# Attention's weights split into float16 halves from the fourth tile of tokens on, and integer additions issued in pieces of 256 columns

## The chip, the core and the metric

The kernel runs on one core of a Trainium2 chip. The metric is device time in microseconds (us): 732.31 us, the median of three runs (731.12 to 734.42). The core's engines each work through a queue of their own, in order: PE (TensorE: matmuls, and PEld, its weight loads), DVE (VectorE), ACT (ScalarE), POOL (GpSimd). SP issues all DMAs here.

## The reference

Attention that keeps the 32 largest scores of a row, followed by two feed-forward layers; batch 2, 8 heads, 576 tokens, head size 64, so 1152 tokens of 512 numbers.

```python
scores = scale * np.matmul(q, k.transpose(0, 1, 3, 2))
kth = np.partition(scores, -top_k, axis=-1)[..., -top_k:-top_k + 1]
scores = np.where(scores >= kth, scores, -1000000000.0)
attn = np.exp(scores - np.max(scores, axis=-1, keepdims=True))
attn = attn / (np.sum(attn, axis=-1, keepdims=True) + 1e-09)
x = np.matmul(attn, v)                      # then [tokens, 512]
h = x @ w_in;  x = np.maximum(0.01 * h, h) @ w_out          # 512 -> 2048 -> 512
h = x @ w2_in; out = (h * np.tanh(softplus(h))) @ w2_out    # 512 -> 2048 -> 512
```

All inputs and the output are float32.

## The kernel before

**Tiles and slots.** The 1152 tokens are nine tiles of 128 (0 to 8). A slot is one head of one tile: 72 slots, in order of tile and then head. Tile 4 holds the end of batch 0 and the start of batch 1, 64 tokens each, so what is a matmul over 128 tokens elsewhere is two over 64 there.

**One slot.** `front` makes the scores (2 halves of 288 columns, L469, into one PSUM bank of `ps_s`) and ACT copies them out (L471). `topk` finds the 32nd largest score on DVE: four MAX8 (L484) and three MATCH_REPLACE8 (L487), each over 576 columns. `weigh` computes three small numbers on POOL (L502 to L506), and ACT makes the masked exponentials `e` (L509, L510). `back` multiplies `e` by V, for which `e` must be transposed:

- `back` in float32 (tiles 0 to 4): PE transposes four blocks of 128 columns into a bank of `ps_pt` (L520), ACT copies them out (L521), PE transposes the last 64 columns (L524), ACT copies those (L525), and five float32 matmuls follow (L529), each recorded as two.
- `back16` (tiles 5 to 8, `T16 = 5`): ACT copies `e` to its float16 half (L542), POOL subtracts for the second half (L543), one DMA transposes both (L546, into `pts`), and PE runs 15 float16 matmuls (L553 to L555). The halves lie in one of two buffers `eh` by turns, 640 columns each, padded with zeros; `pts` comes from the pool `kvp`, which also holds V. This path needs V as float16 halves too: `split_v` makes them in place, per pair of heads, on ACT (squares L124, scaling L363, rounding L365) and POOL (L366). Before, only batch 1's V is split, from slot 34 on (`VX = 34`; `VS = 98` for batch 0 is past the last slot).

**Weights.** The four weight matrices arrive as float32 in 16 groups (`load_w`, slots -1 to 15; `split_w` one slot later), and are brought into a scaled form and float16 halves. A group's first step shifts and joins the words as integers: DVE L209, L212, L215 and L220, and on POOL additions L213 and L218 of 1024 (at the end 512) columns.

**Feed-forward.** A step is `first` (48 matmuls of 128 columns, L609 to L611) of one quarter of a layer for a tile, and `second` (12 of 512 columns, L618 to L620). There are 72 steps; one or two go with a slot from slot 6 on, the rest follow the last slot.

**Order.** The program is written slot by slot with priorities (`at(i, late)`), and a list scheduler with its own timing places every instruction; pools of tiles with few buffers add waits. Pools that matter here: `kvp` with `VB = 5` buffers (V, and `pts` of tiles 5 to 8), `krp` with one, `qp` with one (the queries' float16 halves `qn`, tiles 0 to 4), `sp1` with one (`pts` of `back`). The names `aside` are two scratch rows for `split_v` and for batch 1's K: one lies in the weights' arena, the other is a tile of its own.

Of the kernel before, what the change touches and what calls it, by code (L numbers as in the profile page):

```python
# [18 lines left out]
def topk_attention_moe_moe2_kernel(  # L19
# [34 lines left out]
    VB = 5  # L54
    LV = 0
# [96 lines left out]

    CV = (2, 1, 1, 2, 2, 1, 1, 1, 1, 1, 1, 1, 1, 1, 0, 1)
# [37 lines left out]
    def load_w(q):  # L191
# [4 lines left out]
        for c, n, k0 in stages:  # L196
# [11 lines left out]
            for o, lo, hi in runs:  # L208
                nc.vector.tensor_scalar(out=o, in0=hi, scalar1=3, scalar2=0x3FFFFFFF, op0=ALU.logical_shift_left,  # L209
                                        op1=ALU.bitwise_and)  # L210
                if CV[q] == 2:
                    nc.vector.tensor_scalar(out=hi, in0=hi, scalar1=-0x40000000, scalar2=None, op0=ALU.bitwise_and)  # L212
                    nc.gpsimd.tensor_tensor(out=o, in0=o, in1=hi, op=ALU.add)  # L213
# [90 lines left out]
    def load_kv(src, pool, tag, b, hp):  # L304

        t = pool.tile([P, 2, NB, D], F32, tag=tag, name="raw" + tag)
        nc.sync.dma_start(
            out=t[:, :, 0:4, :],
            in_=src[b, 2 * hp:2 * hp + 2, 0:4 * P, :].rearrange("h (p i) d -> p h i d", i=4))
        for to, at0, n in (((0, S - P, P),) if src is k else ((0, S - SREM, SREM), (SREM, S - P, P - SREM))):  # L310
            nc.sync.dma_start(out=t[to:to + n, :, 4, :],
                              in_=src[b, 2 * hp:2 * hp + 2, at0:at0 + n, :].rearrange("h p d -> p h d"))
        return t

    asides = [warena[:, 4 * NCHW * CH + NB * P:4 * NCHW * CH + NB * P + NB * D],
              cpool.tile([P, NB * D], F32, name="aside")]
# [34 lines left out]
    def split_v(b, hp):  # L351
# [3 lines left out]
        for h in range(2):  # L355
            a = asides[h]
# [3 lines left out]
        for h in range(2):  # L360
            a = asides[h]
# [29 lines left out]
    def prep_q(t, qr):  # L391
# [46 lines left out]
    class Tile_:  # L438
# [11 lines left out]
        def front(self, h):  # L450
# [11 lines left out]
            for half in range(2):  # L462
                where, tag = ((ps_s, "s"), (ps_pt, "pt"))[half if self.t >= SB else 0]
# [48 lines left out]
        def back(self, h):  # L512
# [9 lines left out]
            where, tag = ((ps_pt, "pt"), (ps_g, "g"))[self.t >= TG]  # L522
            pu = where.tile([P, 512], F32, tag=tag, name="pu")
# [8 lines left out]
        def back16(self, h, e):  # L532

            hp, hh = divmod(h, 2)
            if not ehs:
                ehs.append(wh[:, 4 * NCHW * 2 * CH:4 * NCHW * 2 * CH + 2 * SP].rearrange("p (c n) -> p c n", c=2))
                t = krp.tile([P, 2, NB, D], F32, tag="kr", name="eh")
                ehs.append(t.rearrange("p a b c -> p (a b c)").bitcast(F16).rearrange("p (c n) -> p c n", c=2))
                for eh in ehs:
                    nc.gpsimd.memset(eh[:, :, S:], 0.0)  # L540
# [4 lines left out]
            ph = pts.rearrange("p a b c -> p (a b c)").bitcast(F16).rearrange("p (n q) -> p n q", q=P)  # L545
            nc.sync.dma_start(out=ph, in_=eh.rearrange("p c n -> p (c n)"), transpose=True)  # L546
            for b, s, n, p0 in tokens(self.t):
                o = self.av[p0:p0 + n, h * D:(h + 1) * D]
                for i, r in enumerate(R):
                    first, last = i == 0, i == NB - 1  # L550
                    pa, pb = [ph[:r, c * NB + i, p0:p0 + n] for c in range(2)]
                    va, vb = [vsp[b, hp][:r, hh, c, i, :] for c in range(2)]
                    nc.tensor.matmul(o, lhsT=pa, rhs=va, start=first, stop=False)  # L553
                    nc.tensor.matmul(o, lhsT=pa, rhs=vb, start=False, stop=False)
                    nc.tensor.matmul(o, lhsT=pb, rhs=va, start=False, stop=last)  # L555
# [44 lines left out]
    def product_in(m, hi, lo, g, t):  # L600
        where, tag = ((ps_m, "m"), (ps_pt, "pt"))[t >= MB and g == 3]
# [51 lines left out]
    class Layer:  # L653
# [11 lines left out]
        def first(self, g):  # L665
            ph = product_in(2 * self.l, self.hi, self.lo, g, self.t)
# [161 lines left out]
    for i in range(-2, NS):  # L828
# [38 lines left out]
    n = NS  # L867
    while todo or late:
# [33 lines left out]
```

## Time and profile before

| | |
|---|---|
| median of three runs | 732.31 us |
| profiled execution | 732.71 us, of it the span 730.9 us |
| PE busy | 645.2 us (88%) |
| DVE busy | 561.2 us (77%) |
| ACT busy | 541.1 us (74%) |
| POOL busy | 394.0 us (54%) |
| mean granted clock of PE | 0.962 of 2.4 GHz |
| chain that ended last | PE 41%, DVE 23%, ACT 12%, DMA 8% |

The span is the time from the first to the last instruction; 1.8 us of the execution lie outside it. A share of busy time is a mean over stages with different limits, so the stages are to be read apart. They are: the weights with tiles 0 to 2 (until about 285 us), tiles 3 and 4 (until about 423 us), tiles 5 to 8 (until about 630 us), and the feed-forward steps that are left.

### The profile page before, as it was taken

Reading aid. Unit: us, or ns where it says so; the run is one execution under the profiler, and the core shown is the slowest. Engines: PE = TensorE matmul, PEld = TensorE weight load, DVE = VectorE, ACT = ScalarE, POOL = GpSimd, SP = SyncE. Lnnn points to the kernel's source line nnn. Section 1 sums busy time; section 2 is a strip of 40 time slices with the busy share of each in tenths; the row PEclk is TensorE's granted clock in tenths of the full one; section 3 lists DMA queues with packets and bytes.
Section 4 is the critical chain, followed back from the end, with each engine's and each line's share of the span. In section 5 each row is a group of like instructions: output and inputs, shape, how many; then the busy total and the mean of one; then the engine's idle time right before and its main releaser. Section 6 shows DMA issues by size and latency. Waiting matters only on the chain.

```text
span 730.9 us, 16578 instructions
## 1 busy us (share of the span) xinstructions
PE 645.2 (88%) x6428; PEld 464.6 (64%) x6428; DVE 561.2 (77%) x1184; ACT 541.1 (74%) x1056; POOL 394.0 (54%) x550
## 2 busy tenths in 40 slices
PE   2389589888959999899999989998999989999996
PEld 1255345556648776677677757767767767677772
DVE  4998989999899788978687689788889899220112
ACT  5398688888786889877888696786797688663543
POOL 2648855667874754333255465466566557533230
PEclk9999889999976999999999998998999999999998
DMA  8842445351522112002212123233335334310000
GB/s 291 279 163 86 168 167 170 116 155 40 193 90 73 59 37 50 2 23 44 51 36 58 23 54 73 64 69 74 78 60 103 73 57 65 70 30 17 1 16 29
DMA packets 92367, 60.45 MB, mean 83 GB/s; under 512 B 78848, under 2 KB 82944, under 8 KB 92288
## 3 DMA queue, kind: packets, MB, share of 16 engines
q1 hardware_dynamic: 92288, 59.39, 30.1%
q8 instruction: 50, 0.82, 0.5%
q14 instruction: 29, 0.24, 0.1%
HBM read 41.16 MB, written 2.36 MB: 60 GB/s over the span
## 4 chain that ended last, share of the span: by engine, by line
PE 41%; DVE 23%; ACT 12%; issue 8%; DMA 8%; POOL 6%; SPq 1%; POOLq 0%; DVEq 0%; ACTq 0%
DVE top L484 6%; PE ph L609 5%; DVE wk L487 5%; PE ph L610 5%; PE ph L611 5%; PE y L618 5%; PE y L619 5%; PE y L620 5%; PE av L529 3%; PE sps L469 2%; DVE warena L215 2%; DVE warena L209 2%; DMA warena<-in_moe_w_out_dram 2%; DMA pts<-warena 2%; DMA warena<-in_moe_w_in_dram 2%
## 5 line engine op out<-in xcount | busy, mean ns | idle before, releaser
L609 PE MATMUL ph<-xt,warena 128*128 128x128 f16 x1152 | 204.7, 221 | 1.4 <-DMA xt<-xp 1.4
L610 PE MATMUL ph<-xt,warena 128*128 128x128 f16 x1152 | 204.5, 221 | 0.0
L611 PE MATMUL ph<-xt,warena 128*128 128x128 f16 x1152 | 204.5, 221 | 0.0
L484 DVE MAX8 top<-wk 128x8 f32<-128x576 f32 x216 | 157.5, 749 | 1.3
L610 PEld LDWEIGHTS <-warena 128*128 128x128 f16 x1152 | 114.0, 99 | 8.4 <-issue 2.5
L609 PEld LDWEIGHTS <-warena 128*128 128x128 f16 x1152 | 114.3, 99 | 7.9 <-issue 1.1
L618 PE MATMUL y<-warena,gl 128*128 128x512 f16 x288 | 110.9, 385 | 6.0 <-POOL gl L648 2.8
L611 PEld LDWEIGHTS <-warena 128*128 128x128 f16 x1152 | 114.1, 99 | 2.8 <-issue 1.1
L619 PE MATMUL y<-warena,gh 128*128 128x512 f16 x288 | 110.7, 384 | 0.0
L620 PE MATMUL y<-warena,gh 128*128 128x512 f16 x288 | 110.7, 384 | 0.0
L487 DVE MATCH_REPLACE8 wk<-top,wk 128x576 f32<-128x576 f32 x144 | 106.7, 741 | 0.0
L218 POOL TENSOR_TENSOR warena<-warena 128x1024 int32<-128x1024 int32 x26 | 64.1, 2468 | 31.8 <-DVE warena L215 9.1
L509 ACT ACTIVATE wk<-sc,nb,iv 128x576 f32<-128x576 f32 x72 | 62.5, 868 | 20.4 <-POOL nb L502 20.3
L484 DVE MAX8 top<-sc 128x8 f32<-128x576 f32 x72 | 54.0, 750 | 28.6 <-ACT sc L471 27.6
L471 ACT COPY sc<-sps 128x288 f32<-128x288 f32 x144 | 56.9, 395 | 25.0 <-PE sps L469 24.9
L469 PE MATMUL sps<-kst,qst 128*128 128x288 f16 (+1 forms) x320 | 64.7, 304 | 9.5 <-ACT sc L471 5.0
L529 PEld LDWEIGHTS av<-rawkv,pts 128*128 128x128 f32 (+3 forms) x480 | 56.3, 183 | 15.0 <-issue 3.7
L529 PE MATMUL av<-rawkv,pts 128*128 128x64 f32 (+3 forms) x480 | 64.5, 270 | 1.2 <-ACT pts L525 1.2
L502 POOL TENSOR_SCALAR nb<-top,iv 128x1 f32<-128x1 f32 x72 | 21.8, 302 | 80.5 <-DVE top L484 60.1
L645 DVE SCALAR_TENSOR_TENSOR mc<-mc,hs 128x512 f32<-128x512 f32 x36 | 26.1, 725 | 50.4 <-ACT mc L644 50.4
L510 ACT ACTIVATE wk<-wk,nb 128x576 f32<-128x576 f32 x72 | 55.9, 777 | 6.2 <-POOL nb L506 5.9
L632 POOL TENSOR_TENSOR gl<-lk,gh 128x512 f16<-128x512 f32 x36 | 43.6, 1210 | 27.4 <-ACT lk L631 27.0
(179 smaller groups left out, 1481.8 us busy)
## 6 DMA issues: line engine op xcount, KB each, us to landing
warena<-in_moe_w_in_dram SPq DMA_DIRECT2D x16, 1024.0 KB, 5.4
warena<-in_moe_w_out_dram SPq DMA_DIRECT2D x11, 1024.0 KB, 4.9
warena<-in_moe_w_out_dram SPq DMA_DIRECT2D x10, 512.0 KB, 3.4
out_dram<-o SPq DMA_DIRECT2D x9, 256.0 KB, 2.0
qr<-in_q_dram SPq DMA_DIRECT2D x8, 256.0 KB, 3.2
rawkv<-in_v_dram SPq DMA_DIRECT2D x8, 256.0 KB, 2.8
rawkr<-in_k_dram SPq DMA_DIRECT2D x6, 256.0 KB, 3.2
rawkv<-in_k_dram SPq DMA_DIRECT2D x2, 256.0 KB, 7.8
```

The lines of the kernel that those rows point to most:

```text
L218: nc.gpsimd.tensor_tensor(out=o, in0=o, in1=lo, op=ALU.add)
L469: nc.tensor.matmul(sps[p0:p0 + n, :HS], lhsT=lq[:, c, p0:p0 + n], rhs=rk[:, half * HS:(half + 1) * HS], start=(c == 0), stop=(c == 1))
L484: queued(nc.vector.max(out=top[:, 8 * r:8 * r + 8], in_=src))
L487: queued(nc.vector.match_replace(out=wk, in_to_replace=top[:, 8 * r:8 * r + 8], in_values=src, imm_value=NEG))
L509: nc.scalar.activation(e, sc, AF.Prelu, bias=nb[:, 0:1], scale=iv, alpha=1e30)
L529: nc.tensor.matmul(o, lhsT=pts[:r, i, p0:p0 + n], rhs=vst[b, hp][:r, hh, i, :], start=(i == 0), stop=(i == NB - 1))
L609: nc.tensor.matmul(o, lhsT=wb, rhs=xa, start=(c == 0), stop=False)
L610: nc.tensor.matmul(o, lhsT=wa, rhs=xb, start=False, stop=False)
L611: nc.tensor.matmul(o, lhsT=wa, rhs=xa, start=False, stop=(c == KC - 1))
L618: nc.tensor.matmul(y, lhsT=gb, rhs=whi(j), start=(g == 0 and f == 0), stop=False)
L619: nc.tensor.matmul(y, lhsT=ga, rhs=wlo(j), start=False, stop=False)
L620: nc.tensor.matmul(y, lhsT=ga, rhs=whi(j), start=False, stop=(g == FG - 1 and f == 3))
```

## The change

- `T16` goes from 5 to 3: tiles 3 and 4, 16 slots, take `back16`. Batch 0's V is therefore split too, at slots 18 to 24 (`VS = 18`), and batch 1's from slot 30 on (`VX = 30`).
- In `back16` the two halves lie without padding, the last 64 columns of both in one block, so that the DMA moves 9 blocks of 128 instead of 10 and a head has 14 matmuls instead of 15; POOL's subtraction becomes two instructions. In tiles 3 and 4 (`TK = 5`) there is one `eh` and one `pts` (of `sp1`); from tile 5 on `eh` alternates between two as before, and `pts` comes from `kvp`.
- `kvp` has 6 buffers instead of 5. Room for it comes from `aside`: its second row is now the buffer `qn` of the queries.
- POOL's integer additions are issued in pieces of 256 columns (`add`).
- `SB` goes from 99 to 3: from tile 3 on the second half of a head's scores uses a bank of `ps_pt`, as it does for the very first head. The feed-forward uses that bank for its fourth quarter only once the last slot has been written (`over`), not from tile 7 on.

```diff
-    VB = 5
-    LV = 0
+    VB = 6
+    LV = 2
+    PIECE = 256
+    def add(o, x):
+        for a in range(0, o.shape[1], PIECE):
+            nc.gpsimd.tensor_tensor(out=o[:, a:a + PIECE], in0=o[:, a:a + PIECE], in1=x[:, a:a + PIECE], op=ALU.add)
...
-                    nc.gpsimd.tensor_tensor(out=o, in0=o, in1=lo, op=ALU.add)
+                    add(o, lo)
...
-    asides = [warena[:, 4 * NCHW * CH + NB * P:4 * NCHW * CH + NB * P + NB * D],
-              cpool.tile([P, NB * D], F32, name="aside")]
+    def aside(h):
+        if h:
+            return qp.tile([P, 6 * P], F16, tag="qn", name="aside").bitcast(F32)[:, :NB * D]
+        return warena[:, 4 * NCHW * CH + NB * P:4 * NCHW * CH + NB * P + NB * D]
...
-                where, tag = ((ps_s, "s"), (ps_pt, "pt"))[half if self.t >= SB else 0]
+                where, tag = ((ps_s, "s"), (ps_pt, "pt"))[half if self.t >= SB or (self.t, h) == (0, 0) else 0]
...
         def back16(self, h, e):
-            eh = ehs[h % 2]
-            nc.scalar.copy(eh[:, 0, :S], e)
-            nc.gpsimd.tensor_tensor(out=eh[:, 1, :S], in0=e, in1=eh[:, 0, :S], op=ALU.subtract)
-            pts = kvp.tile([P, 2, NB, D], F32, tag="kv", name="pts")
+            if self.t < TK or h % 2:
+                eh = wh[:, 4 * NCHW * 2 * CH:4 * NCHW * 2 * CH + 2 * S]
+            else:
+                if not ehs:
+                    ehs.append(krp.tile([P, 2, NB, D], F32, tag="kr", name="eh"))
+                eh = ehs[0].rearrange("p a b c -> p (a b c)").bitcast(F16)[:, :2 * S]
+            nc.scalar.copy(eh[:, :S], e)
+            nc.gpsimd.tensor_tensor(out=eh[:, S + SREM:], in0=e[:, :4 * P], in1=eh[:, :4 * P], op=ALU.subtract)
+            nc.gpsimd.tensor_tensor(out=eh[:, S:S + SREM], in0=e[:, 4 * P:], in1=eh[:, 4 * P:S], op=ALU.subtract)
+            if self.t < TK:
+                pts = sp1.tile([P, NB, P], F32, tag="pts", name="pts").rearrange("p a b -> p (a b)")
+            else:
+                pts = kvp.tile([P, 2, NB, D], F32, tag="kv", name="pts").rearrange("p a b c -> p (a b c)")
...
-    T16 = 5
-    TG = 5
-    VS = 98
-    VX = 34
+    T16 = 3
+    TK = 5
+    VS = 18
+    VX = 30
...
-    SB = 99
+    SB = 3
```

Three places in the order of the instructions. First POOL at the weights' first groups; L213 and L218 are the additions, L158 is the line of `add`. Before:

```order
L455 TENSOR_SCALAR iv<-ki,qi 128x2
L458 TENSOR_SCALAR iv<-iv 128x2
L213 TENSOR_TENSOR warena<-warena 128x1024
L218 TENSOR_TENSOR warena<-warena 128x1024
L213 TENSOR_TENSOR warena<-warena 128x1024
L218 TENSOR_TENSOR warena<-warena 128x1024 x2
L455 TENSOR_SCALAR iv<-ki,qi 128x2
L218 TENSOR_TENSOR warena<-warena 128x1024
```

With the change:

```order
L465 TENSOR_SCALAR iv<-ki,qi 128x2
L468 TENSOR_SCALAR iv<-iv 128x2
L158 TENSOR_TENSOR warena<-warena 128x256 x20
L465 TENSOR_SCALAR iv<-ki,qi 128x2
L158 TENSOR_TENSOR warena<-warena 128x256 x4
L468 TENSOR_SCALAR iv<-iv 128x2
```

Five additions of 1024 columns became twenty of 256 in the same place.

Second, ACT at the fifth and sixth head of tile 3. Line numbers of the change stand 10 to 16 higher. Before, with the two copies per head (L521, L525):

```order
L509 ACTIVATE wk<-sc,nb,iv 128x576
L521 COPY pts<-pt 128x512
L510 ACTIVATE wk,sums<-wk,nb 128x576
L430 COPY qst<-qt 128x1024
L471 COPY sc<-sps 128x288
L630 ACTIVATE gh<-ph,fac_1115 128x512
L631 ACTIVATE lk<-ph,fac_1115 128x512
L686 ACTIVATE o<-y,ivo 128x512
L525 COPY pts<-pu 64x128
```

With the change (L551 is the copy to float16):

```order
L702 ACTIVATE o<-y,ivo 128x512
L519 ACTIVATE wk<-sc,nb,iv 128x576
L551 CAST warena<-wk 128x576
L520 ACTIVATE wk,sums<-wk,nb 128x576
L124 ACTIVATE qn,qpart<-qr 128x512
L646 ACTIVATE gh<-ph,fac_1180 128x512
L647 ACTIVATE lk<-ph,fac_1180 128x512
L519 ACTIVATE wk<-sc,nb,iv 128x576
L417 ACTIVATE qn<-qr,qs 128x4x64
L551 CAST warena<-wk 128x576
```

The second CAST writes the same part of `warena` as the first, which the DMA transpose reads in between; six other instructions stand between the two.

Third, SP at tile 3. `kst` are the transposes of batch 1's K, `pts` those of the weights. Before:

```order
L307 DMA rawkr<-in_k_dram 128x2x256
L311 DMA rawkr<-in_k_dram 128x2x64
L340 DMA_TRANSPOSE kst<-warena 128x4x128
L342 DMA_TRANSPOSE kst<-warena 128x64
L340 DMA_TRANSPOSE kst<-aside 128x4x128
L342 DMA_TRANSPOSE kst<-aside 128x64
```

With the change:

```order
L559 DMA_TRANSPOSE pts<-warena 128x9x128
L398 DMA qr<-in_q_dram 64x8x64 x2
L559 DMA_TRANSPOSE pts<-warena 128x9x128 x2
L350 DMA_TRANSPOSE kst<-warena 128x4x128
L559 DMA_TRANSPOSE pts<-warena 128x9x128
L352 DMA_TRANSPOSE kst<-warena 128x64
L350 DMA_TRANSPOSE kst<-aside 128x4x128
L352 DMA_TRANSPOSE kst<-aside 128x64
```

Sixteen transposes of `pts` now stand among the loads and transposes of batch 1's K and the queries.

## Rows read from the trace of the kernel before

**Rows 1.** Windows: us, then busy us (instructions) per engine, clock, DMA, GB/s.
```profile
20.00:240.00 220.00, 172.79 (x1204) 117.99 (x1205) 208.69 (x409) 170.28 (x302) 145.26 (x146) 0.91 0.41 138
240.00:420.00 180.00, 174.58 (x1833) 131.08 (x1831) 143.10 (x333) 145.19 (x324) 83.88 (x154) 1.00 0.16 39
420.00:625.00 205.00, 195.41 (x2328) 145.02 (x2327) 181.47 (x386) 160.50 (x321) 126.08 (x205) 0.97 0.36 69
```

**Rows 2.** Instructions by line, DVE, 10 to 262 us: busy us, mean ns | idle.
```profile
L209 DVE TENSOR_SCALAR warena<-warena 128x1024 int32<-128x1024 int32 (+1 forms) x30 | 35.6, 1187 | 7.6 <-PE lp L256 2.8 <-DMA warena<-in_moe_w_in_dram 2.4 <-DMA warena<-in_moe_w_out_dram 2.3
L215 DVE SCALAR_TENSOR_TENSOR warena<-warena 128x1024 int32<-128x1024 int32 (+1 forms) x24 | 33.6, 1401 | 0.2
...
L212 DVE TENSOR_SCALAR warena<-warena 128x1024 int32<-128x1024 int32 x6 | 7.0, 1168 | 0.1
```

**Rows 3.** Timeline of DVE: start us, us, instruction [idle before].
```profile
12.45 0.69 DVE L209 TENSOR_SCALAR warena<-warena 128x1024 int32<-128x1024 int32 x1 [1.29 <-DMA warena<-in_moe_w_in_dram]
...
23.05 1.23 DVE L215 SCALAR_TENSOR_TENSOR warena<-warena 128x1024 int32<-128x1024 int32 x1
...
71.38 2.89 DVE L209 TENSOR_SCALAR warena<-warena 128x1024 int32<-128x1024 int32 x1
```

**Rows 4.** Line L218 on POOL: ns min/median/max, first and last start.
```profile
L218 POOL TENSOR_TENSOR warena<-warena x26: 2369/2397/2847, 16.4 to 191.2; 128x1024 int32<-128x1024 int32 x26
L218 POOL TENSOR_TENSOR wraw<-wraw,warena x8: 1289/1302/1626, 194.3 to 255.7; 128x512 int32<-128x512 int32 x8
```

**Rows 5.** Timeline of PE, tile 3: `back` in float32.
```profile
328.20 0.27 PE L524 MATMUL pu<-identf,wk 128*64 128x128 f32 x1
328.31 1.00 PE L529 MATMUL av<-rawkv,pts 128*128 128x64 f32 x8
329.15 0.22 PE L610 MATMUL ph<-xt,warena 128*128 128x128 f16 x1
...
330.44 0.43 PE L529 MATMUL av<-rawkv,pts 64*128 64x64 f32 x2
330.80 0.66 PE L520 MATMUL pt<-identf,wk 128*128 128x128 f32 x4
331.30 0.22 PE L611 MATMUL ph<-xt,warena 128*128 128x128 f16 x1
```

**Rows 6.** Timeline of PE, tile 5: the 15 matmuls of `back16`, first and next.
```profile
445.20 0.19 PE L553 MATMUL av<-rawkv,pts 128*128 128x64 f16 x1
...
445.84 0.23 PE L609 MATMUL ph<-xt,warena 128*128 128x128 f16 x1
```

**Rows 7.** Instructions by line, ACT, whole span.
```profile
L521 ACT COPY pts<-pt 128x512 f32<-128x512 f32 x40 | 23.3, 583 | 10.5 <-PE pt L520 10.0 <-PE av L529 0.3
L542 ACT CAST warena<-wk 128x576 f16<-128x576 f32 x16 | 10.8, 673 | 0.1
L525 ACT COPY pts<-pu 64x128 f32<-64x128 f32 x40 | 10.3, 258 | 10.1 <-PE pu L524 10.0
L363 ACT ACTIVATE warena<-rawkv,vs 128x320 f32<-128x320 f32 x4 | 2.3, 573 | 0.0
L124 ACT ACTIVATE warena<-rawkv 128x320 bf16<-128x320 f32 x4 | 1.9, 470 | 1.7 <-DMA rawkv<-in_v_dram 1.3 <-DVE top L484 0.4
L365 ACT CAST rawkv<-warena 128x320 f16<-128x320 f32 x4 | 1.8, 461 | 0.0
```

**Rows 8.** Timeline of ACT: exponentials of the first head of tiles 3 and 5.
```profile
284.93 0.76 ACT L510 ACTIVATE wk<-wk,nb 128x576 f32<-128x576 f32 x1
...
423.36 0.78 ACT L510 ACTIVATE wk<-wk,nb 128x576 f32<-128x576 f32 x1
```

**Rows 9.** DMA issues: count, median us to landing.
```profile
pts<-warena SPq DMA_TRANSPOSE x16, 3.5
```

**Rows 10.** Instructions by line, POOL: the subtraction of `back16`.
```profile
L543 POOL TENSOR_TENSOR warena<-wk,warena 128x576 f16<-128x576 f32 x16 | 21.6, 1348 | 22.6 <-ACT warena L542 22.3
```

**Rows 11.** Waits, 420 to 625 us: who <- for whom: us, times, longest.
```profile
PEld L553 <- DMA pts<-warena: 9.5, 7, 3.0
```

More of the change, by code (lines that the diff above doesn't have):

```diff
@@ L212, in load_w @@
                     nc.vector.tensor_scalar(out=hi, in0=hi, scalar1=-0x40000000, scalar2=None, op0=ALU.bitwise_and)
-                    nc.gpsimd.tensor_tensor(out=o, in0=o, in1=hi, op=ALU.add)
+                    add(o, hi)
                 else:
@@ L309, in load_kv @@
             in_=src[b, 2 * hp:2 * hp + 2, 0:4 * P, :].rearrange("h (p i) d -> p h i d", i=4))
-        for to, at0, n in (((0, S - P, P),) if src is k else ((0, S - SREM, SREM), (SREM, S - P, P - SREM))):
+        for to, at0, n in (((0, S - P, P),) if src is k else ((0, S - SREM, SREM), (SREM, S - SREM, SREM))):
             nc.sync.dma_start(out=t[to:to + n, :, 4, :],
@@ L355, in split_v @@
         for h in range(2):
-            a = asides[h]
+            a = aside(h)
             squares(raw[:, h].rearrange("p i d -> p (i d)"), part[:, h:h + 1], a.bitcast(BF16)[:, :NB * D])
@@ L360, in split_v @@
         for h in range(2):
-            a = asides[h]
+            a = aside(h)
             r = raw[:, h].rearrange("p i d -> p (i d)")
@@ L400, in prep_q @@
             else:
-                qn = qp.tile([P, 4, 3, D], F16, tag="qn", name="qn").rearrange("p a b c -> p (a b c)")
+                qn = qp.tile([P, 6 * P], F16, tag="qn", name="qn")
             if not c:
@@ L521, in back @@
             nc.scalar.copy(pts[:, 0:4, :], pt)
-            where, tag = ((ps_pt, "pt"), (ps_g, "g"))[self.t >= TG]
-            pu = where.tile([P, 512], F32, tag=tag, name="pu")
+            pu = ps_pt.tile([P, 512], F32, tag="pt", name="pu")
             nc.tensor.transpose(pu[:SREM, :P], e[:, 4 * P:S], identf)
@@ L534, in back16 @@
             hp, hh = divmod(h, 2)
[L535 to L540, printed above, removed]
-            eh = ehs[h % 2]
-            nc.scalar.copy(eh[:, 0, :S], e)
@@ L543, in back16 @@
-            nc.gpsimd.tensor_tensor(out=eh[:, 1, :S], in0=e, in1=eh[:, 0, :S], op=ALU.subtract)
-            pts = kvp.tile([P, 2, NB, D], F32, tag="kv", name="pts")
-            ph = pts.rearrange("p a b c -> p (a b c)").bitcast(F16).rearrange("p (n q) -> p n q", q=P)
-            nc.sync.dma_start(out=ph, in_=eh.rearrange("p c n -> p (c n)"), transpose=True)
+            if self.t < TK or h % 2:
[4 more added lines that the diff above has]
+                eh = ehs[0].rearrange("p a b c -> p (a b c)").bitcast(F16)[:, :2 * S]
@@ L547, in back16 @@
+            ph = pts.bitcast(F16)[:, :2 * S].rearrange("p (n q) -> p n q", q=P)
+            nc.sync.dma_start(out=ph, in_=eh, transpose=True)
             for b, s, n, p0 in tokens(self.t):
                 o = self.av[p0:p0 + n, h * D:(h + 1) * D]
[L549 to L555, printed above, removed]
+                va, vb = vsp[b, hp][:, hh, 0], vsp[b, hp][:, hh, 1]
+                for i in range(4):
+                    pa, pb = ph[:, i, p0:p0 + n], ph[:, 5 + i, p0:p0 + n]
+                    nc.tensor.matmul(o, lhsT=pa, rhs=va[:, i, :], start=(i == 0), stop=False)
+                    nc.tensor.matmul(o, lhsT=pa, rhs=vb[:, i, :], start=False, stop=False)
+                    nc.tensor.matmul(o, lhsT=pb, rhs=va[:, i, :], start=False, stop=False)
+                nc.tensor.matmul(o, lhsT=ph[:, 4, p0:p0 + n], rhs=va[:, 4, :], start=False, stop=False)
+                nc.tensor.matmul(o, lhsT=ph[:SREM, 4, p0:p0 + n], rhs=vb[:SREM, 4, :], start=False, stop=True)
@@ L598, in transposed, with product_in @@
         return hi, lo, xi
-    def product_in(m, hi, lo, g, t):
-        where, tag = ((ps_m, "m"), (ps_pt, "pt"))[t >= MB and g == 3]
+    over = []
+    def product_in(m, hi, lo, g):
+        where, tag = ((ps_m, "m"), (ps_pt, "pt"))[bool(over) and g == 3]
         ph = where.tile([P, 512], F32, tag=tag, name="ph")
@@ L665, in first @@
         def first(self, g):
[L666 removed]
+            ph = product_in(2 * self.l, self.hi, self.lo, g)
             beside = nc.vector if FG * self.t + g >= TF[self.l] else nc.gpsimd
@@ L857, in topk_attention_moe_moe2_kernel @@
             for bp in ((0, (i - VS) // 2), (1, (i - VX) // 2)):
-                if bp in vst and bp not in vsp and T16 < NTT:
+                if bp in vst and bp not in vsp:
                     split_v(*bp)
@@ L867, in topk_attention_moe_moe2_kernel @@
     n = NS
+    over.append(True)
     while todo or late:
```

3 lines of the change are left out of this document (1 added, 2 removed).

## The prediction

> **What bounds the kernel now.** I read the busy time of the engines by stage first, then the costliest lines within a stage, then the timeline at the places that the change touches, and last the waits. The kernel has three bounds, one after the other. From 20 to 240 us DVE is busy 208.69 of 220 us, ACT 170.28 and PE 172.79 at a granted clock of 0.91 [rows 1]: DVE sets the pace there. From 240 to 420 us PE is busy 174.58 of 180 us at the full clock, ACT 145.19, DVE 143.10. From 420 to 625 us PE is busy 195.41 of 205, DVE 181.47. After the last slot only feed-forward steps are left, whose number the change leaves as it is. So what DVE saves before 240 us moves everything after it forward, and what PE saves after 240 us comes off the end, as far as ACT and DVE can follow.
>
> In the first stage DVE's busy time is not all work. Its shift L209 takes 0.69 us when POOL is idle and 2.89 us at 71.38 us, and the join L215 takes 1.23 us undisturbed [rows 3]. POOL's addition of 1024 columns takes 2.397 us [rows 4]. A DVE instruction that meets one waits until it is over. The Trainium skill (SBUF — State Buffer, "Who interferes with whom") says why: the two engines share a pair of ports, and the first one holds it for its whole instruction. The trace agrees: the longest L209 is its own 0.69 us and less than one addition more.
>
> **The change part by part.**
>
> *Additions in pieces.* What DVE stands: 30 L209 took 35.6 us where 30 x 0.69 = 20.7 would do, 24 L215 33.6 instead of 24 x 1.23 = 29.5, six L212 (the same shape as L209) 7.0 instead of 4.1 [rows 2, 3]. That is 14.9 + 4.1 + 2.9 = 21.9 us, rather too little, since the few narrower instructions among them are counted as wide ones. A wait lasts in proportion to the addition that it meets. An addition of 512 columns takes 1.302 us and one of 1024 2.397 [rows 4], so 0.21 us are fixed, and one of 256 should take about 0.75 us (an estimate from these two rows). The waits shrink to 0.75/2.40 = 31%, and DVE saves 0.69 x 21.9 = 15 us. POOL pays for it: four pieces take 3.0 us instead of 2.4, and of the 32 additions of 1024 columns each costs 0.6 us more, of the 8 of 512 about 0.2, together 21 us, on an engine that is busy 145.26 of 220 us there. DVE without the 15 us would be busy 194 us, still ahead of ACT's 170, so most of it should come through: I take 12. The ends: 5 us lost, if a quarter of POOL's 21 us is waited for, to 18 gained, with the narrow instructions that I left out.
>
> The Trainium skill (GPSIMD Engine Reference, "2.1 Instruction dispatch") speaks against pieces: each POOL instruction pays for a dispatch in software. The trace shows that as the fixed 0.21 us; the sum has it in POOL's 21 us already, and a rival below is built on it.
>
> *Tiles 3 and 4 in float16 halves.* In the timeline of tile 3 a head costs PE the time from one start to the next: 0.11 us for the last transpose (328.20 to 328.31), 0.84 and 0.36 for the ten float32 matmuls, 0.50 for four transposes (330.80 to 331.30), together 1.81 us [rows 5]. The 15 float16 matmuls of tile 5 take 0.64 us (445.20 to 445.84) [rows 6]; 14 should take 0.60. A head saves 1.21 us. Tile 4 has the same transposes and twice the matmuls on either side; I give it the same saving. 16 x 1.21 = 19.4 us of a PE that is busy 97% of this stage. ACT is next. Per head it loses two copies and gains one: 0.583 + 0.258 - 0.673 = 0.17 us, 2.7 us in all [rows 7]. The four new splits of V cost it 2 x (0.470 + 0.573 + 0.461) = 3.0 us each, 12.0 us [rows 7]. So ACT has 145 + 9 = 154 us to do in 180 - 19 = 161 us, 96%. An engine that works in order and waits on three others will not do that, and I take half of PE's saving, 10 us. The ends: 19 us gained, and a loss that the last rival prices.
>
> POOL's new subtractions (16 x 1.348 = 21.6 us [rows 10], and some 0.2 us for each one's second piece) lie in a stage where it is busy 83.88 of 180 us [rows 1]; that hides them. The splits' own 8 x 2 subtractions go the same way. The sixteen transposes lie on SP ahead of loads of batch 1's K, which is fetched slots ahead of its use; I cost the queue at nothing. Without that cover a late K would hold a slot for one landing, 3.5 us [rows 9].
>
> *Tiles 5 to 8.* One matmul less is 32 x 0.04 = 1 us of PE. With two free buffers for `pts`, a transpose no longer waits until PE has read the one before. PE waited 9.5 us for these transposes [rows 11], and the clock of this stage, 0.97 on the mean [rows 1], cost 0.03 x 205 = 6 us. Most of such a wait is the landing (3.5 us [rows 9]), which stays. I take 2 us, between nothing and 15.
>
> *The rest.* A second bank for scores spares PE and ACT a part of their turns; the third bank of the feed-forward is given up in tiles 7 and 8. I take 1 us for both, between -3 and 5. The scratch row shared with the queries makes a split and a `prep_q` wait for each other; these are written slots ahead, and I cost it at nothing, at worst 3 us.
>
> The sum: 12 + 10 + 1 + 2 + 1 = 26 us. The profiled execution took 732.7 us (span 730.9, 1.8 outside), 0.4 above the median of 732.3, so 706.3 to 706.7; I say 706.
>
> **The rivals.**
>
> *POOL eats the pieces' gain.* Weights are only multiplied once POOL has added them, and POOL now takes 21 us longer over them, with DVE's instructions between the pieces. For it: POOL's 145 us become 166, as much as ACT has. Against: POOL is still idle a quarter of the stage. The first term vanishes: 706 + 12 = 718, at its worst end 723.
>
> *ACT becomes the bound of tiles 2 to 4.* The 12 us of new splits fall into slots 18 to 24, before PE's saving. For it: the 96% above. Against: the feed-forward's part on ACT can lag some slots. The 10 us vanish: 716. With the rival before: 728, which is no change.
>
> *Everything arrives.* DVE's 18, PE's 19, and 10 from the waits of tiles 5 to 8: about 732 - 18 - 19 - 10 = 685.
>
> *The single buffers make a convoy: slower.* In tiles 3 and 4 one `eh` and one `pts` serve all heads. A head's copy (0.67), subtraction (1.35) and landing (3.5) must be over before the next copy may start: 5.5 us [rows 7, 9, 10], and ACT and SP stand still behind a copy or a transpose that waits. The order shows two copies with only six instructions of ACT between them. Now 16 heads take 423.36 - 284.93 = 138.4 us, 8.65 each [rows 8]. At a period of 9.65 us (138.4 + 16 over 16) the change's other 16 us are gone; at 11 us the 16 heads take 37.6 us longer, and the time is 732 - 16 + 38 = 754. Against: 5.5 us fits into 8.65 with 3 us to spare, and tiles 5 to 8 run the same steps with one `pts` already.
>
> *The change doesn't do what it says* has no case here: the order shows 32 and 8 additions cut up and 16 heads moved.
>
> **How the numbers follow.** The forecast of 706 (694 to 712) has 0.50; POOL eats the gain 0.15 (718); ACT becomes the bound 0.13 (716); both 0.05 (728); everything arrives 0.09 (685); the convoy 0.08 (754). Differences within 0.5% (728.6 to 736.0) can't be told from none here. Faster takes the forecast, the two single rivals and the best case, 0.87, less 0.02 for waits that I left out; same has the double rival, which lies on the border, and 0.01 of those waits, 0.06; slower the convoy and the other 0.01, 0.09. The range that holds 8 in 10: from 688, leaving out part of the best case, to 728, leaving out the convoy.
>
> **What would show it.** Right: L209 and L215 near their undisturbed times, with none above about 1.5 us; the first head of tile 3 some 10 us earlier than 284.93; tiles 3 and 4 in about 128 us; DVE below 200 us in the first stage. Wrong: L209 still at 1.2 us on the mean; ACT's copies to float16 standing before a DMA, or PE at the new matmuls, for more than 1 us per head; PE's clock below 1.00 in tiles 3 and 4; or the first stage as long as before with POOL in place of DVE.

## The result, and the profile after

The changed kernel took 741.05 us (median of four runs, 736.84 to 744.42) against 731.74 for the kernel before on the same chip: a ratio of 1.0124, 95% interval 1.0094 to 1.0154. It is slower by 9 us where 706 was forecast. The profiled run took 744.42 us, its span is 742.6; it is the slowest of the four, so what its trace adds up to lies some 3 us above the median.

The windows view of the changed kernel (columns as in [rows 1]) with the stretches of [rows 1] and the time after them:

```profile
20.00:240.00 220.00, 175.60 (x1207) 117.31 (x1204) 190.12 (x404) 170.06 (x303) 173.62 (x243) 0.89 0.42 140
240.00:420.00 180.00, 164.28 (x1804) 118.92 (x1803) 136.29 (x328) 149.21 (x329) 109.13 (x183) 0.97 0.28 59
420.00:625.00 205.00, 186.16 (x2206) 137.22 (x2206) 183.18 (x403) 159.17 (x321) 129.94 (x239) 0.97 0.38 68
625.00:750.00 125.00, 109.94 (x1178) 76.47 (x1175) 23.13 (x48) 59.35 (x99) 38.06 (x46) 0.98 0.10 23
```

And the last stretch of the kernel before, which ahead of the prediction was not shown:

```profile
625.00:750.00 125.00, 98.70 (x1050) 68.13 (x1047) 18.87 (x41) 53.65 (x90) 32.28 (x37) 0.97 0.11 24
```

Read DVE first, the third of the busy times. In the first stretch it fell from 208.69 to 190.12 us, and yet PE did 1207 matmuls there, hardly more than before (1204): almost nothing reached the engine that has the most left to do. From 240 to 625 us PE stood idle 15.7 + 18.8 = 34.6 us, where it had stood 15.0. The matmuls that it missed there are in the last row: 1178 after 625 us instead of 1050. The whole account is short: PE was busy 645.2 us and idle 85.7 of the span before, and is busy 641.5 and idle 101.1 now. The busy time that should have fallen by 20 us fell by 3.7, and the idle time grew by 15.4. It did not grow in the first stage: from 0 to 240 us PE was idle 63.5 us before and 58.9 now, and busy 4.6 us longer for 13 matmuls more.

The waits view tells what PE waited for (us in total, times, the longest). The kernel before, 0 to 240 us:

```profile
PE kt L345 <- DVE kn L337: 12.0, 4, 7.0
...
PE qt L428 <- DVE qn L408: 5.1, 2, 3.2
...
PE gram L231 <- POOL warena L218: 4.1, 7, 1.0
```

The changed kernel, the same stretch:

```profile
PE gram L238 <- POOL warena L158: 13.8, 16, 3.7
PE kt L355 <- DVE kn L347: 6.8, 4, 1.9
...
PE qt L438 <- DVE qn L418: 1.2, 2, 0.6
```

What DVE delivers earlier (keys and queries, 9 us less waiting) POOL delivers later (the weights' additions, 10 us more). Now 240 to 625 us, before:

```profile
PE av L553 <- DMA pts<-warena: 7.6, 6, 2.7
```

and after:

```profile
PE av L565 <- DMA pts<-warena: 10.1, 10, 2.3
PE av L565 <- DMA pts<-eh: 7.3, 4, 2.3
PE ph L625 <- DVE u L100: 3.5, 3, 2.8
PE tot L119 <- ACT warena L124: 1.8, 1, 1.8
PE tot L119 <- ACT wk L519: 1.7, 1, 1.7
```

PE waits 10 us more for the transposing DMAs of the halves. Its other waits in this stretch sum to 17 us, where they were 7; the last row shown is a split's (`tot`). The same waits divided by tiles, first tiles 3 and 4 (285 to 434 us), then tiles 5 to 8 (434 to 645 us):

```profile
PE av L565 <- DMA pts<-warena: 4.9, 5, 1.5
```

```profile
PE av L565 <- DMA pts<-eh: 7.8, 5, 2.3
PE av L565 <- DMA pts<-warena: 5.2, 5, 2.3
```

Only 4.9 us are at the new halves of tiles 3 and 4. Tiles 5 to 8, which were in halves before, wait 13.0 us instead of 7.6.

The first stage's lines on DVE and POOL, 10 to 262 us (busy us, mean ns | idle before), answer to [rows 2]:

```profile
L222 DVE SCALAR_TENSOR_TENSOR warena<-warena 128x1024 int32<-128x1024 int32 (+1 forms) x24 | 32.9, 1371 | 0.0
L216 DVE TENSOR_SCALAR warena<-warena 128x1024 int32<-128x1024 int32 (+1 forms) x30 | 25.0, 833 | 8.9 <-DMA warena<-in_moe_w_in_dram 7.0 <-PE lp L263 1.7 <-DMA warena<-in_moe_w_out_dram 0.2
...
L219 DVE TENSOR_SCALAR warena<-warena 128x1024 int32<-128x1024 int32 x6 | 5.5, 925 | 0.1
```

```profile
L158 POOL TENSOR_TENSOR warena<-warena 128x256 int32<-128x256 int32 x128 | 105.3, 855 | 19.3 <-DVE warena L219 6.2 <-ACT warena L260 5.7 <-PE kt L357 2.6
```

and the source view of that POOL line (ns: least, median, most; first and last start) answers to [rows 4]:

```profile
L158 POOL TENSOR_TENSOR warena<-warena x128: 718/736/1796, 14.2 to 197.9; 128x256 int32<-128x256 int32 x128
```

The shift came down from 1187 to 833 ns, the join hardly moved (1401 to 1371). The prediction's three lines of DVE together gave back 12.8 us (76.2 to 63.4). A piece takes 0.736 us in the median, close to the estimate of 0.75, but 0.855 on the mean and up to 1.80. POOL's wide additions took 64.1 + 14.5 = 78.6 us and now take 105.3, 27 more.

Next, the exponentials of the first heads of tiles 3 and 5, in ACT's timeline of the changed kernel:

```profile
292.38 0.77 ACT L520 ACTIVATE wk<-wk,nb 128x576 f32<-128x576 f32 x1
...
426.50 0.79 ACT L520 ACTIVATE wk<-wk,nb 128x576 f32<-128x576 f32 x1
```

and before, the first head of tile 5:

```profile
411.84 0.78 ACT L510 ACTIVATE wk<-wk,nb 128x576 f32<-128x576 f32 x1
```

The row at 423.36 in [rows 8] is that tile's second head, so the prediction's 8.65 us a head was 7.93 (284.93 to 411.84, 16 heads). Now it is 8.38. The sign "tiles 3 and 4 in about 128 us" therefore stood for no gain: they took 126.9 us before, and take 134.1 now. Slot 24 starts 7.5 us later, not 10 earlier: at slot 22 the changed kernel was still 11 us ahead (259.75 against 270.80), and then lost it. ACT's timeline there shows how:

```profile
259.75 0.78 ACT L520 ACTIVATE wk<-wk,nb 128x576 f32<-128x576 f32 x1
...
260.67 0.56 ACT L373 ACTIVATE warena<-rawkv,vs 128x320 f32<-128x320 f32 x1
261.13 0.55 ACT L373 ACTIVATE aside<-rawkv,vs 128x320 f32<-128x320 f32 x1
261.59 0.45 ACT L375 CAST rawkv<-warena 128x320 f16<-128x320 f32 x1
261.93 2.56 ACT L275 ACTIVATE wraw<-wraw,w_s 128x512 f32<-128x512 f32 x4
264.39 0.45 ACT L375 CAST rawkv<-aside 128x320 f16<-128x320 f32 x1
...
268.98 0.64 ACT L124 ACTIVATE qn<-qr 128x512 bf16<-128x512 f32 x1
...
282.57 0.77 ACT L520 ACTIVATE wk<-wk,nb 128x576 f32<-128x576 f32 x1
```

and DVE's timeline has the other end of it:

```profile
269.75 0.15 DVE L100 TENSOR_SCALAR u<-qpart 128x1 int32<-128x1 int32 x1 [6.51 <-ACT qn L124]
```

From slot 22 to slot 23 pass 22.8 us. ACT is busy 20.3 of them, but works off a split and the weights' last rounding before the queries of tile 3 (`qn`), for which DVE stands 6.51 us.

### The profile page after: what moved, and what is told of

Its sections match the earlier page's. It is cut to its first block, busy times and chain, and to the rows that moved or that the text cites. A ratio compares the mean times of both kernels' runs of the same rounds, so it can differ in the third digit from the quotient of the medians.

```text
span 742.6 us, 16867 instructions
## 1 busy us (share of the span) xinstructions
PE 641.5 (86%) x6420; PEld 453.7 (61%) x6420; DVE 541.5 (73%) x1199; ACT 549.7 (74%) x1072; POOL 457.7 (62%) x724
## 5 line engine op out<-in xcount | busy, mean ns | idle before, releaser
L634 PE MATMUL y<-warena,gl 128*128 128x512 f16 x288 | 112.7, 391 | 6.9 <-POOL gl L664 2.6
L158 POOL TENSOR_TENSOR warena<-warena 128x256 int32<-128x256 int32 x128 | 105.3, 855 | 19.3 <-DVE warena L219 6.2
L635 PE MATMUL y<-warena,gh 128*128 128x512 f16 x288 | 112.5, 391 | 0.0
L636 PE MATMUL y<-warena,gh 128*128 128x512 f16 x288 | 112.2, 390 | 0.0
L481 ACT COPY sc<-sps 128x288 f32<-128x288 f32 x144 | 53.2, 395 | 11.3 <-PE sps L479 10.9
L663 POOL TENSOR_SCALAR gh<-mc 128x512 f16<-128x512 f32 x32 | 20.1, 628 | 56.4 <-DVE mc L661 46.6
L497 DVE MATCH_REPLACE8 wk<-top,sc 128x576 f32<-128x576 f32 x72 | 53.4, 742 | 0.0
L263 PE MATMUL lp<-warena,diag 128*128 128x512 f32 x80 | 49.4, 703 | 3.0 <-POOL diag L258 2.2
```

The source lines that it names most:

```text
L158: nc.gpsimd.tensor_tensor(out=o[:, a:a + PIECE], in0=o[:, a:a + PIECE], in1=x[:, a:a + PIECE], op=ALU.add)
L481: nc.scalar.copy(sc[:, half * HS:(half + 1) * HS], sps[:, :HS])
L497: queued(nc.vector.match_replace(out=wk, in_to_replace=top[:, 8 * r:8 * r + 8], in_values=src, imm_value=NEG))
L634: nc.tensor.matmul(y, lhsT=gb, rhs=whi(j), start=(g == 0 and f == 0), stop=False)
L635: nc.tensor.matmul(y, lhsT=ga, rhs=wlo(j), start=False, stop=False)
L636: nc.tensor.matmul(y, lhsT=ga, rhs=whi(j), start=False, stop=(g == FG - 1 and f == 3))
```

## The experiments

All ran in three rounds beside the kernel before (medians 730.7 to 731.5 in the different sets); differences below are those of the ratios, times 731 us. The theories in the expectations: A, the scratch row in the queries' buffer makes splits and queries wait for each other; B, the new splits in slots 18 to 24 cost the loss; D, the halves' own chain in tiles 3 and 4 gives PE's saving back as waits; P, pieces only change what PE waits for.

**Is it the shared row?** Two kernels free the queries' buffer of the second scratch row: `aside_one` uses the first row for both heads, `row_in_k` takes batch 0's from the keys' pool.

```diff
 def aside(h):
-    if h:
-        return qp.tile([P, 6 * P], F16, tag="qn", name="aside").bitcast(F32)[:, :NB * D]
     return warena[...]
```

> The changed kernel with one edit: head 1's scratch row for the splits and for batch 1's K is head 0's row, so nothing of it lies in the queries' buffer any more. Theory A (the shared buffer: the queries of tile 3 are prepared only after the first split has left the buffer, and DVE stands still for want of scores at 262 to 276 us): the preparation of tile 3's queries starts some 20 us earlier than 269 us, the gap of 22.8 us between the exponentials of slots 22 and 23 falls below 12, and the time is 720 to 731. Theory B (the splits' own 12 us of ACT work, in a stage where ACT is full): the gap stays above 18 us and the time within 4 us of 741. Theory C (the single buffers of tiles 3 and 4 make a convoy): the gap in tile 2 may go, but tiles 3 and 4 stay at 140 us and the time above 735.

```diff
+        if not b:
+            row = ksp.tile([P, 2, S], F16, tag="kst", name="aside")...
-            a = aside(h)
+            a = row if h and not b else aside(h)
```

> The changed kernel with one edit: the four splits of batch 0 take head 1's scratch row from the pool of K's transposes, so only batch 1's K and splits still share the queries' buffer. Theory A: as far as the loss comes from batch 0's splits ahead of tile 3's queries, the gap between the exponentials of slots 22 and 23 (22.8 us) falls below 12 and the time to 725 to 733; what remains of the gaps at slots 31 and 36 (17 and 21 us) belongs to batch 1's use of the buffer. Theory B: gap and time as in the changed kernel, 737 to 745. Theory C: 735 or more, with the gap gone.

Measured 745.11 (1.0201, 1.0162 to 1.0240) and 745.12 (1.0200, 1.0176 to 1.0225): both slower still. The gap between slots 22 and 23 fell to 17.4 us in `aside_one` and stayed at 22.8 in `row_in_k`: theory A falls, and no theory had said that the kernels would be slower still. `aside_one` started slot 24 at 282.1 us, 10 earlier than the changed kernel, but slot 40 at 440.0, 13.5 later. So the shared row is not the cause, and an early slot 24 was worth nothing by itself.

The reverse, the kernel before with its second row in the queries' buffer and nothing else:

```diff
-    asides = [warena[...], cpool.tile([P, NB * D], F32, name="aside")]
+    def aside(h):
+        if h:
+            return qp.tile([P, 6 * P], F16, tag="qn", name="aside").bitcast(F32)[:, :NB * D]
+        return warena[...]
```

> The kernel before with one edit: head 1's scratch row is the queries' buffer. Here batch 0 is not split, so the buffer is shared by the queries of tile 4 and batch 1's K and splits alone. Theory A: slots 22 to 24 stay as before, since nothing uses the row there; a loss of 0 to 8 us appears about slots 28 to 40: 732 to 740. Theories B and C: no difference, 732 within 2.

725.97 (0.9928, 0.9908 to 0.9948): 5 us faster, which none of the theories had. Its last stretch (windows view):

```profile
625.00:750.00 125.00, 90.08 (x954) 62.57 (x954) 18.71 (x37) 47.16 (x78) 27.07 (x31) 0.98 0.07 14
```

96 matmuls fewer than before are left at 625 us, though no instruction was taken away.

**The pieces.** The changed kernel with whole additions, the kernel before with pieces alone, and, further below, each again on another base:

```diff
-        for a in range(0, o.shape[1], PIECE):
-            nc.gpsimd.tensor_tensor(out=o[:, a:a + PIECE], ...)
+        nc.gpsimd.tensor_tensor(out=o, in0=o, in1=x, op=ALU.add)
```

> The changed kernel with the integer additions whole again (1024 and 512 columns). If the pieces give what the head of tile 2 showed (its exponentials came 5.5 us earlier), the time is 5 to 6 us above the changed kernel's, 746 to 747, and DVE is busy some 18 us longer before 240 us. If POOL eats all of it further on, the time is 741 within 3. If the pieces are what costs (POOL is busy 174 of 220 us with them), it is below 737.

```diff
+    def add(o, x):
+        for a in range(0, o.shape[1], 256): ...
-                    nc.gpsimd.tensor_tensor(out=o, in0=o, in1=hi, op=ALU.add)
+                    add(o, hi)
```

> The kernel before with the additions in pieces of 256 columns and nothing else. Theory P (pieces only change what PE waits for in the first stage: its waits for DVE's normalised keys and queries shrink by about 10 us, its waits for POOL's additions grow by as much, and the gram's matmuls, fed piece by piece, keep PE busy some 6 us longer): between before + 1 and before + 6 us, about 735, slot 16 some 6 us earlier, PE's matmuls up to 240 us not more than before's 1226. Rival (the prediction's term: what DVE saves moves all that follows): before - 10, about 721.

`whole_adds`: 739.93 (1.0118, 1.0099 to 1.0137), no measurable difference from the changed kernel: in it the pieces are worth nothing. Nor are they what brought its slots forward: with whole additions slot 16 starts at 212.1 us, with pieces at 213.8. `pieces`: 728.12 (0.9944, 0.9924 to 0.9965), 4 us faster than before: my theory P said slower, and the prediction's term said 10. P's waits came: those for DVE's keys and queries fell from 19.1 to 7.6 us, the gram (the sum over a weight group that gives its scale) kept PE busy 34.4 us instead of 28.3, and the wait for POOL rose. But PE had done 1294 matmuls by 240 us, not at most 1226, and slot 16 came 15 us earlier, not 6. The wait for POOL and the window, 0 to 240 us:

```profile
PE gram L238 <- POOL warena L158: 14.7, 12, 3.7
```

```profile
0.00:240.00 240.00, 184.36 (x1294) 126.84 (x1295) 204.03 (x437) 188.43 (x337) 183.99 (x265) 0.91 0.45 154
```

**Tiles 3 and 4, taken apart.** Four kernels make a square: halves or not, splits of batch 0's V or not.

```diff
-    T16 = 3
+    T16 = 5
-    VS = 18
-    VX = 30
+    VS = 98
+    VX = 34
-    SB = 3
+    SB = 5
```

> The changed kernel with attention's weights of tiles 3 and 4 left in float32 (T16 = 5, no splits of batch 0's values, second score bank from tile 5 on); pieces, six buffers and the shared row stay. Theory D (the halves of tiles 3 and 4 lost what they should have gained: the PE time they save comes back as PE waits, and the feed-forward steps left over end the program later): about 728 us, slots 24 and 40 near 279 and 412 us, PE idle between 240 and 625 us back to 15 us or less, clock 1.00 there. Rival E (the rest of the change, the pieces and the shared row, set the loss and tiles 3 and 4 are neutral): 738 to 742 us.

> As t5, with the weights' integer additions whole again: the change without its two main parts. Theory D: 726 to 732 us, no more than 3 us from t5, since pieces measured nothing beside the halves. Rival F (pieces pay once the halves don't eat the gain): 4 us or more slower than t5.

```diff
 # t5, and:
-    VS = 98
+    VS = 18
-            half = r.bitcast(F16)...
+            half = (r.bitcast(F16) if b else wh[:, 4 * NCHW * 2 * CH:...])...
```

> As t5, plus the splits of batch 0's values at slots 18 to 24, with the halves written to a scratch row that nobody reads: their work on ACT, DVE and POOL without the halves' attention. Theory B (the splits in slots 18 to 24 are what costs): 736 us or more, 8 us or more above t5. Theory D proper (the halves' own chain in tiles 3 and 4): at most 4 us above t5.

```diff
 # the changed kernel, and:
-    VS = 18
+    VS = 98
-                va, vb = vsp[b, hp][:, hh, 0], vsp[b, hp][:, hh, 1]
+                if b: ...
+                else:
+                    va, vb = [kst[b, hp][:, hh, c:c + NB * D]... for c in (0, S - NB * D)]
```

> The changed kernel with its halves in tiles 3 and 4 but without the splits of batch 0's values: for batch 0 the matmuls of tiles 3 and 4 read the transposed keys as if they were the values' halves, and v_i is 1. Theory B: 730 us or less, since the splits' 12 us of ACT and the late third query tile are gone. Theory D proper (the halves' chain of cast, subtraction and transposing DMA): 736 us or more, with PE's waits for the DMA of tiles 3 and 4 as in the changed kernel.

| | time | ratio (95%) | slot 24 | PE busy, idle |
|---|---|---|---|---|
| t5_whole | 732.29 | 1.0018 (1.0003 to 1.0034) | 284.7 | 640.5, 90.0 |
| t5 | 737.41 | 1.0078 (1.0054 to 1.0101) | 279.9 | 651.4, 83.2 |
| splits_only | 739.97 | 1.0125 (1.0092 to 1.0158) | 292.7 | 647.8, 87.5 |
| no_split | 737.83 | 1.0077 (1.0053 to 1.0100) | 281.3 | 638.1, 96.3 |
| changed kernel | 741.05 | 1.0124 (1.0094 to 1.0154) | 292.4 | 641.5, 101.1 |

The square is not quite clean: the two kernels with halves also have the second score bank in tiles 3 and 4 (`SB`) and batch 1's splits four slots earlier (`VX`). With and without halves, the splits cost 3.4 us (1.0078 to 1.0125, 1.0077 to 1.0124; the intervals overlap at their ends, but both pairs agree). They hold slot 24 back by 11 to 13 us, of which only these 3.4 reach the end. The halves without splits are worth nothing, within some 2 us: in `no_split` PE is busy 13 us less than in `t5`, and idle 13 us more (one profiled run each). Busy time is itself no pure count of work: `t5` and `t5_whole` have the same matmuls and differ by 10.9 us. The largest wait of `no_split` from 240 to 625 us:

```profile
PE av L569 <- DMA pts<-warena: 12.7, 8, 5.8
```

B falls (8 us and more for the splits, 730 or less without them). D holds for both of these kernels, but not for `t5`, which is 9 us above its 728 and nearly at rival E's 738: halves and splits together are less than half of the loss there, and the rest of the change has some of it. `t5_whole` is 4.4 us faster than `t5`, where D said 3 at most and F said slower: on this base the pieces cost time.

**Does the size of a piece matter, and do the banks?**

```diff
 # t5, and:
-    PIECE = 256
+    PIECE = 512
```

> t5 with pieces of 512 columns instead of 256: 64 pieces for the wide additions, each 1.302 us undisturbed, so POOL's extra work is a third of that of 256. Theory P: PE's wait for POOL between nothing (t5_whole, 1 us) and 15 us (t5), and a time between t5_whole's 732 and t5's 737, about 734. Rival (the loss has nothing to do with the pieces' size, only with the order that any cut makes): 737 again, or above.

```diff
 # t5_whole, and:
-    where, tag = (...)[half if self.t >= SB or (self.t, h) == (0, 0) else 0]
+    where, tag = (...)[half if self.t >= SB else 0]      # SB = 99
-    where, tag = ((ps_m, "m"), (ps_pt, "pt"))[bool(over) and g == 3]
+    where, tag = ((ps_m, "m"), (ps_pt, "pt"))[t >= MB and g == 3]      # MB = 7
```

> t5_whole with the banks as before: one bank for scores, the fourth transposes' bank and the feed-forward's third bank from tile 7 on as before. It differs from shared_row (726 us) then only in the sixth buffer and the 14 matmuls. Theory H (the banks lost the 6 us between the two): 726 to 728 us. Rival (the sixth buffer and its earlier loads, or only another order): 731 or more.

`t5_512`: 731.99 (1.0017, 0.9991 to 1.0042), which is no measurable change from the kernel before and 4.5 us below `t5`. So the rival falls: pieces of 256 columns lose on this base, pieces of 512 lose nothing against whole ones. But P's price does not explain it, for PE's wait for POOL is nearly all there with 512 already (1.0 us in `t5_whole`, 15.3 in `t5`):

```profile
PE gram L238 <- POOL warena L158: 12.8, 8, 3.3
```

`old_banks`: 731.01 (0.9994, 0.9970 to 1.0017); so the banks lose some 2 us, within the intervals, and H falls: the 5 us between it and `shared_row` belong to the sixth buffer, the 14 matmuls, or the order that they make.

**Later matmuls.** The matmuls of a head's `back16` are written one slot later, so that other work stands between the DMA and them:

```diff
-            for b, s, n, p0 in tokens(self.t): ...matmuls...
+            def products(): ...the same matmuls...
+            pending.append(products)
+            if h == H - 1:
+                flush()
...
         at(i, 0.5)
+        flush()
```

> The changed kernel with the matmuls of each head in halves written one slot later, so that the order puts other work of PE between the transposing DMA and them. Theory D (PE's waits for the transposing DMA, 10 us more than before, are what eats the saving of tiles 3 and 4): PE's waits for these DMAs from 240 to 625 us fall from 17 us to 8 or less, and the time to about 732. Rival G (the wait moves elsewhere, to the copies and subtractions in front of the single buffers, and the feed-forward steps still come late): 739 or more, with less wait at these matmuls.

> after_late with whole additions. Theory D (the later place of the halves' matmuls is worth 7 us whatever else is in the kernel): 733 us, 7 below whole_adds, PE's waits for the transposing DMAs near 10 us instead of 13. Rival (a chance order): 738 or more.

`after_late`: 734.11 (1.0029, 1.0010 to 1.0048), 7 us faster than the changed kernel; `late_whole`: 730.38 (0.9991, 0.9973 to 1.0008), 9 us faster than `whole_adds`. Twice the same step, twice a gain well outside the intervals; D's 732 was missed by 2 us, G falls. The waits of PE in `after_late`, 240 to 625 us, against 10.1 and 7.3 above:

```profile
PE av L566 <- DMA pts<-eh: 5.4, 4, 2.0
PE av L566 <- DMA pts<-warena: 5.2, 6, 2.1
```

They fell by 7 us to 10.6, where D had 8 or less. Most of that is in tiles 5 to 8 (13.0 to 6.9 us), little in tiles 3 and 4 (4.9 to 3.7). PE's idle time is 85.9 us, as in the kernel before. In `late_whole` the DMA waits hardly differ from those of `whole_adds` (11.1 and 12.9 us), so there most of the gain is the order's.

**How much is the order alone?**

```diff
-    LEAD = 5.0
+    LEAD = 4.0
```

> The kernel before with the feed-forward steps due 4 slots after their own instead of 5: the same instructions, no byte and no column more or less, in another order. If a new order alone moves the time by some us, as the parts' changing values suggest: 3 us or more from 731, on either side, with PE's work at full clock within 2 us of before's 624. Rival (the order matters little, the parts have their own values): 730 to 733.

> shared_row with the additions in pieces of 256 columns as well. If the parts have values of their own, shared_row's -5 and the pieces' -3 add up: about 723 us, the best so far. Rival (order by chance: the two gains are not of the parts): anywhere from 724 to 736, with the first stage's waits of PE for POOL's additions near 15 us and those for DVE near 18 as in every kernel with pieces.

`lead4`: 734.21 (1.0044, 1.0026 to 1.0063): 3 us slower with the very same instructions. (PE's busy time times the granted clock, added up over windows of 20 us, came to 614 and not to the 623 of the kernel before: that sum is no measure to 2 us, and I use busy and idle time instead.) `shared_pieces`: 726.20 (0.9916, 0.9880 to 0.9953): the gains of its two parts don't add up. It and `shared_row` are the fastest versions; their intervals overlap.

## Why the prediction was wrong

*What bounds the kernel.* "What DVE saves before 240 us moves everything after it forward" is the first step that failed. Slots did move: 5.5 us at slot 16, 11 at slot 22, though `whole_adds` shows them as early without the pieces. But a slot that starts early does not end the program; PE's matmuls do, and from 20 to 240 us it did 1207 of them, where it had done 1204. The changed kernel took 9 us of waits for DVE from PE and gave 10 for POOL, and the gram kept PE busy 6.8 us longer. The rival "POOL eats the pieces' gain" had the mechanism; it priced the gain away, and in the changed kernel so it came. On the kernel before the same exchange left PE 68 matmuls further at 240 us and the end 4 us earlier.

*Pieces, -12 us.* DVE's saving of 15 was 12.8 in the three lines that it was worked out from (18.6 in the whole stage), POOL's price of 21 was 27. Worth to the whole: -4.1 on the kernel before, -0.9 with `shared_row`, +0.4, +2.8 and +4.4 in the changed kernel, `late_whole` and `t5_whole`. No base gave 12.

*Tiles 3 and 4, -10 us.* This is the largest miss. The cost of a head on PE was right. In the timeline of the changed kernel, tile 3:

```profile
301.54 0.20 PE L565 MATMUL av<-rawkv,pts 128*128 128x64 f16 x1
...
302.16 0.42 PE L479 MATMUL sps<-kst,qst 128*128 128x288 f16 x2
```

0.62 us where 0.60 was expected. What failed is the step from there to the end: "what PE saves after 240 us comes off the end, as far as ACT and DVE can follow". I asked whether the other engines had room, and not where PE would next stand still. The 13 us of busy time that `no_split` saves against `t5` came back as 13 us of idle time. That PE now follows a chain of copy, subtraction, landing and matmuls per head, and stands where its fixed order puts the matmuls close behind the landing, is shown for a part of it: the waits for the landings are 10 us longer in the changed kernel, half of that in tiles 3 and 4 and half in tiles 5 to 8. Writing the matmuls a slot later gave 7 and 9 us back, but the waits for the landings fell by 7 us in one case and by 2 in the other. The rest of the idle time lies in shorter waits for ACT and DVE, whose cause stays open. On top come the splits, 3.4 us: the rival "ACT becomes the bound" put them at slots 18 to 24, where they are, but priced them at the loss of a gain and not at a loss (3.4 us is no more than a new order alone can move, see `lead4` and `shared_row`). From `t5_whole` to `whole_adds` halves and splits together are +7 us, from `t5` to the changed kernel +3.4.

*The convoy.* It was to make ACT and SP stand. ACT's wait was 6.9 us over 16 heads, 0.43 each, and the heads took 8.38 us, not 11. With the same single buffers `after_late` has back 7 of the 9 us that the change lost, so the buffers are not the main thing. SP did stand, 28.8 us from 285 to 430 us before transposes whose buffer PE had still to read; in `after_late` it stands 41.5 us there. It did not hold up batch 1's K: PE waited 0.2 us for `kst` from 240 to 625 us, so on that side the queue was rightly costed at nothing.

*The clock.* It fell from 1.00 to 0.97 in tiles 3 and 4, one of the named signs. An instance is PE's timeline of the changed kernel at 296 us:

```profile
295.74 0.39 PE L634 MATMUL y<-warena,gl 128*128 128x512 f16 x1 [1.46 <-POOL gl L664]
295.97 0.38 PE L635 MATMUL y<-warena,gh 128*128 128x512 f16 x1
...
297.58 0.63 PE L634 MATMUL y<-warena,gl 128*128 128x512 f16 x1
298.00 0.63 PE L635 MATMUL y<-warena,gh 128*128 128x512 f16 x1
```

Matmuls of 512 columns that followed each other every 0.23 us follow every 0.42 from then on. The windows view of 296 to 300 us has the granted clock, with the change and before:

```profile
296.00:300.00 4.00, 4.00 (x12) 1.61 (x11) 3.93 (x7) 3.94 (x8) 3.74 (x7) 0.57 0.14 28
```

```profile
296.00:300.00 4.00, 2.99 (x42) 2.65 (x42) 3.39 (x6) 3.57 (x9) 1.78 (x2) 1.00 0.02 4
```

0.57 is nearly the lower of its two levels (1.2 of 2.4 GHz), and PE was busy all 4 us for 12 matmuls. What made it fall is not shown: PE had waited 0.30 us before 293.57 and 1.46 before 295.74, but the kernel before waits 1.06 us before 295.28 and 1.01 before 297.43 and stays at 1.00. Such stretches are one reason why PE's busy time fell by 3.7 us and not by 20: 0.03 of the 164 us of that stage is some 5 us (an estimate). The gram's 6.8 us are another.

*The rest, -4 us in all.* `t5_whole` holds all of it but the second score bank in tiles 3 and 4, and stands at +1.3 us. The shared scratch row, "costed at nothing", is no loss: alone it gained 5.

*What stays open.* `lead4` and `shared_row` show that another order of the same instructions is worth 3 to 5 us either way. The values of single parts below that, the splits' 3.4 us among them, why pieces gain on one base and lose on the other, and the 5 us between `shared_row` and `old_banks` are not settled. Nor was the later place of the matmuls tried on the kernel before, whose PE waits 7.6 us for the landings in tiles 5 to 8: how much of its 7 to 9 us belongs to the change is open.

## What to carry to other kernels

When one engine has the most work left at the end, count what a change does to that engine's idle time, by what releases it, and not to the start of the stages. Work that is taken off it comes off the end only if the engine does not wait as long elsewhere: look for the next wait, and try the consumer of a DMA later behind its landing. With a list scheduler, measure first what a neutral edit moves; terms below that can't be forecast or credited one by one.

## What the runs showed of the hardware

POOL and DVE stretch each other: with pieces DVE's shifts came down from 1187 to 833 ns, but a POOL piece of 0.736 us took up to 1.80. The six pieces above 1.3 us (1.71 to 1.80) all run beside a join of DVE (L222). A DMA transpose of 9 blocks of 128 landed in the median 3.3 us from the arena and 2.8 from `eh` (10 blocks: 3.5 from the arena [rows 9], 3.0 from `eh`):

```profile
pts<-warena SPq DMA_TRANSPOSE x32, 3.3
pts<-eh SPq DMA_TRANSPOSE x16, 2.8
```

The gram's matmuls that are fed piece by piece keep PE busy longer for the same 274 instructions: 28.32 us from 20 to 240 us before, 35.15 after (windows view of that tile alone):

```profile
20.00:240.00 220.00, 35.15 (x274) 5.35 (x30) 7.39 (x45) 0.89 0.42 140
```

A single matmul takes as long as before (246 and 251 ns on the mean), so they overlap each other less. The lines view from 10 to 262 us, before and after:

```profile
L231 PE MATMUL gram<-warena 128*128 128x128 bf16 x224 | 20.7, 246 | 8.0 <-POOL warena L218 4.1 <-DVE warena L220 3.4 <-DVE u L100 0.3
```

```profile
L238 PE MATMUL gram<-warena 128*128 128x128 bf16 x224 | 27.2, 251 | 18.5 <-POOL warena L158 13.8 <-DVE u L100 4.4 <-DVE x0s L103 0.2
```
